# V of a batch loaded once, for its range and for its splits

## The chip, the cores and the metric

The kernel runs on one core of a Trainium2 chip. The metric is device time in microseconds of one execution; the kernel before takes 630.58 us (median of 3 runs, 629.67 to 632.43). The engines have the profile's names: PE (TensorE matmuls; PEld its weight loads), DVE (VectorE), ACT (ScalarE), POOL (GpSimd), SP (the queue that issues nearly all DMAs). Each engine works through its own instructions in the order in which the program lists them, and waits where an operand or a buffer isn't free.

## The reference

Attention with 8 global and 96 local keys and a bias per head (4 batches, 8 heads, 768 positions, 64 per head), then a feed-forward layer on its output. All arrays are float32.

```python
scores = q @ k.transpose(0, 1, 3, 2) / sqrt(D) + bias     # masked to global and local keys
a = softmax(scores);  x = a @ v                           # x -> (3072 tokens, 512)
h = x @ w_in                                              # 512 -> 2048
out = (maximum(h, 0) + alpha * minimum(h, 0)) @ w_out     # 2048 -> 512
```

## The kernel before

**Units.** The 3072 tokens are cut into 12 units u of 256 tokens; units 3b, 3b+1 and 3b+2 make batch b. A unit runs attention for 8 heads (scores `sp`, biased scores `pr` on DVE at L717, exponentials on ACT at L722, products with V `av` at L789), turns its output `xn` into the transposed fp16 pair `xt` (L819), and runs 16 slices f of the feed-forward layer: 12 matmuls `h` (L851), a chain of four operations that makes `g` (ACT L349, DVE L873, ACT L875, DVE L375) and 6 matmuls `o` (L896) that add to the output. Attention of later units is interleaved with the feed-forward of earlier ones. The names carry their numbers: h4_9 is unit 4, slice 9; pt5_1 is unit 5, head 1; xt4 belongs to unit 4.

**Split numbers.** fp32 operands are fed to PE as two fp16 halves (high, and what is left). From unit 2 on V is split too (`load_v`): V of a unit is loaded as `rawv` (two DMAs of 256 KB), multiplied by a scale vs of the batch, and split into `v16` (ACT or DVE at L349/L350 for the high half, DVE at L376 for the low one). Copies of shifted rows, `gp`, are made from `v16` by DMAs (L637).

**The range.** vs is a power of two, found by `v_range` from the largest |V| of the batch: all of V is loaded (six DMAs of 256 KB for batches 1 to 3, into the two `stage` buffers, L456), ACT takes the sums of absolute values (L458, tile `vr`), DVE their maximum (L464, `vmm`), DVE spreads it on a diagonal (L468, `vdg`), PE multiplies that with ones (L470, `vrow`, which gives every partition all 128 maxima), DVE reduces the product (L472), and seven small DVE operations make vs and the output scale osc (L477 to L483). The last four steps have one key. So V of batches 1 to 3 is read from HBM twice.

**What sets the order.** Nothing is written in order by hand: every operation has a key (in slices: 16 per unit) and a modelled cost; `Plan.order` simulates the five engines, and at each moment starts the ready operation with the lowest key on each engine (some operations may go to another engine when the first is behind, `FLEX`). `LAG` is what it adds from the end of one engine's work to the start of what waits for it; for a DMA (SP) 1100 ns. `behind` makes an operation wait in the plan for an earlier one. Each tag in `BUFS` has so many buffers; `rw` (17 of 4 KB a partition) holds raw weights, raw V, `v16`, `gp`, and the `g` of units 3 and later. The program is then emitted in the simulated order, and on the chip each engine keeps it.

Of the kernel before, what the change touches and what calls it, by code (L numbers as in the profile page):

```python
# [20 lines left out]
ALU = mybir.AluOpType  # L21
# [3 lines left out]
P = 128  # L25
# [114 lines left out]
class Plan:  # L140
# [37 lines left out]
    def order(self):  # L178
# [34 lines left out]
        while events:  # L213
# [11 lines left out]
            for e in engines:  # L225
# [35 lines left out]
                heapq.heappush(events, (busy, i, "busy"))  # L261
                heapq.heappush(events, (end + self.LAG[e], i, "free"))
                for j in after[i]:
                    need[j] -= 1
                    for x in engines:
                        own = x == e and e != "SP"
                        at[j][x] = max(at[j][x], end + ((0 if e == "PE" else 60) if own else self.LAG[e]))
# [24 lines left out]
def c_dma(nbytes):  # L292
    return nbytes / 360.0
# [21 lines left out]
WLEAD = 8  # L315
VLEAD = 26.5
VS = 5
# [12 lines left out]
def fast(tc, cn, a):  # L330
    nc = tc.nc
    ctx = ExitStack()
    with ctx:
# [51 lines left out]
        def buf(tag, name, shape, dtype=F32):  # L385
            return Buf(plan, pools[tag], tag, shape, dtype, name)
# [54 lines left out]
        alpha_ = [SimpleNamespace(t=ak.t[:, f : f + 1]) for f in range(NF)]  # L441

        def v_range(b, key):
            m = buf("vm", f"vm{b}", [P, 6])
            for i in range(3):

                t = [buf("w", f"vr{b}_{i}", [P, 2, 512])] * 2 if not b else [
                    buf("stage", f"vr{b}_{i}_{j}", [P, 512]) for j in range(2)]
                if not b:
                    op("SP", key, c_dma(P * 4096), lambda t=t, i=i: nc.sync.dma_start(  # L450
                        out=t[0].t, in_=a["v"][b, 2 * i : 2 * i + 2].rearrange("j p d -> p j d")), w=[t[0]])
                for j in range(2):
                    k = key + 2 * i + j if b else VR
                    x = (lambda t=t, j=j: t[j].t) if b else (lambda t=t, j=j: t[j].t[:, j, :])
                    if b:
                        op("SP", k, c_dma(P * 2048), lambda x=x, i=i, j=j: nc.sync.dma_start(  # L456
                            out=x(), in_=a["v"][b, 2 * i + j]), w=[t[j]])
                    op("ACT", k, c_act(512, ptr=1), lambda x=x, i=i, j=j: nc.scalar.activation(  # L458
                        out=x(), in_=x(), func=AF.Abs, accum_out=m.t[:, 2 * i + j : 2 * i + j + 1]),
                       r=[], w=[(t[j], j), (m, 2 * i + j)])  # L460
            if not b:
                key = VR - 5
            e = buf("vmm", f"vmm{b}", [P, 4])
            op("DVE", key + 6, 80, lambda: v.tensor_reduce(out=e.t[:, 0:1], in_=m.t, axis=AX.X, op=ALU.max), r=[m], w=[e])  # L464

            dg = buf("wf", f"vdg{b}", [P, 3, P])
# [17 lines left out]

            op("DVE", key + 6, 1150, scale, r=[e], w=[vs[b], osc[b]])

# [119 lines left out]
        def load_v(u, key):  # L606
# [5 lines left out]
            def load(name, parts):  # L612
                raw = buf("rw", "raw" + name, [P, 1024])
                for part, rows, j, src in parts:
                    op("SP", key, c_dma(P * 4096 // len(parts)), lambda rows=rows, j=j, src=src: nc.sync.dma_start(
                        out=raw.t.rearrange("p (j k) -> p j k", j=2)[rows, j], in_=src), w=[(raw, part)])
                x = buf("rw", name, [P, 1024])
                for j in range(2):
                    in_ = lambda j=j: raw.t[:, 512 * j : 512 * j + 512]
                    hi, lo = (lambda j=j: view(x)[:, j, 0]), (lambda j=j: view(x)[:, j, 1])  # L620
                    k = key + VS + 0.1 * j
                    mul(k, hi, in_, vs[b], [raw, vs[b]], [(x, (j, 0))], "ACT", 512)
# [505 lines left out]
```

## Time and profile before

| | |
|---|---|
| median of 3 runs | 630.58 us |
| the profiled execution | 631.23 us; its span 629.4 us |
| PE busy | 606.6 us (96%) |
| DVE, ACT, POOL busy | 450.8 (72%), 404.5 (64%), 59.9 us (10%) |
| mean granted clock of PE | 0.994 |
| DMA | 98.78 MB, mean 157 GB/s |

The span runs from the first to the last instruction; 1.8 us of the execution lie around it. A share of busy time is an average over stages: DVE is at 72% over the whole span, and without a gap in one stretch of it. In a timeline row the bracket at the end is the idle time of that engine just before, with what ended it by the profile.

### The profile page before, as it was taken

To read this page: it belongs to the slowest core of one execution; us is meant where nothing else is said; L and a number is where in the kernel's file an instruction comes from. 1 tells how busy PE (TensorE), PEld (TensorE's weight loads), DVE (VectorE), ACT (ScalarE), POOL (GpSimd) and SP (SyncE) were. 2 spreads that over 40 slices of the span, in tenths; PEclk is the share of its full clock that TensorE was granted. 3 is DMA by queue.
4 is the path that set the end of the run, shared out by engine and by line. 5 is a ranking of instruction groups with operands and counts; after the bars stand their busy time and mean duration, and the time that the engine had idled before them with its cause. 6 is when DMAs were issued, how large, how long until landed. Compare 5 with 4: busy or idle time off the path is not lost.

```text
span 629.4 us, 13874 instructions
## 1 busy us (share of the span) xinstructions
PE 606.6 (96%) x5124; PEld 416.7 (66%) x5124; DVE 450.8 (72%) x1318; ACT 404.5 (64%) x1049; POOL 59.9 (10%) x137
## 2 busy tenths in 40 slices
PE   8899999989999999898999999999999999999995
PEld 6787666556667666565666666676666676676663
DVE  5599999995777587585677777787677677656431
ACT  5999999955647466554665775675666665543431
POOL 2001233322111000000000000000000000000000
PEclk9999999999999999998999999999999999999998
DMA  8998664456455655976569558859549647431001
GB/s 310 410 407 270 207 131 107 123 119 156 99 114 130 135 132 153 227 127 153 148 145 216 170 132 179 219 157 194 163 122 195 180 101 139 131 68 34 34 2 39
DMA packets 128844, 98.78 MB, mean 157 GB/s; under 512 B 103168, under 2 KB 103424, under 8 KB 128768
## 3 DMA queue, kind: packets, MB, share of 16 engines
q1 hardware_dynamic: 128624, 97.69, 60.9%
q8 instruction: 42, 0.69, 0.4%
q14 instruction: 34, 0.28, 0.1%
q10 hardware_dynamic: 144, 0.13, 0.1%
HBM read 62.92 MB, written 6.29 MB: 110 GB/s over the span
## 4 chain that ended last, share of the span: by engine, by line
PE 76%; DVE 11%; DMA 7%; issue 2%; ACT 2%; POOL 0%; SPq 0%; ACTq 0%; DVEq 0%; POOLq 0%
PE o L896 32%; PE h L851 32%; PE av L789 5%; PE sp L679 4%; DMA vr<-in_v_dram 2%; DVE wf L533 2%; DVE whl L376 2%; PE sp L711 2%; DMA w<-in_w_dram 1%; DVE whl L538 1%; DVE g L873 1%; DMA rawgp<-in_v_dram 1%; DVE pr L717 1%; DMA pt<-ps 1%; DVE ps L376 1%
## 5 line engine op out<-in xcount | busy, mean ns | idle before, releaser
L851 PE MATMUL h<-xt,whl 128*128 128x256 f16 x2304 | 282.7, 273 | 4.8 <-DVE g L873 4.1
L851 PEld LDWEIGHTS <-whl 128*128 128x128 f16 x2304 | 223.2, 98 | 63.1 <-issue 8.3
L896 PE MATMUL o<-whl,g 128*128 128x512 f16 x864 | 209.0, 380 | 0.0
L349 ACT ACTIVATE g<-h,ak 128x256 f32<-128x256 f32 x170 | 79.7, 469 | 130.6 <-PE h L851 130.3
L873 DVE SCALAR_TENSOR_TENSOR g<-h,g 128x256 f32<-128x256 f32 x192 | 80.4, 420 | 106.5 <-ACT g L349 105.6
L896 PEld LDWEIGHTS <-g 128*128 128x128 f16 x864 | 82.3, 98 | 79.8 <-ACT g L349 5.9
L722 ACT ACTIVATE pr<-pr,sm 128x256 f32<-128x256 f32 (+1 forms) x192 | 92.2, 483 | 4.4 <-DVE sm L717 4.4
L875 ACT CAST g<-g 128x256 f16<-128x256 f32 x144 | 57.6, 400 | 41.7 <-DVE g L873 41.5
L375 DVE TENSOR_TENSOR g<-g 128x256 f16<-128x256 f32 x144 | 60.5, 420 | 30.2 <-ACT g L875 30.1
L717 DVE CUSTOM_DVE_ANT_0 pr<-sp,D 128x256 f32<-128x256 f32 (+1 forms) x192 | 67.4, 394 | 6.2 <-PE sp L711 5.1
L896 PE MATMUL o<-whl,gh 128*128 128x512 f16 x192 | 57.2, 379 | 0.0
L376 DVE SCALAR_TENSOR_TENSOR ps<-pr,ps 128x512 f16<-128x512 f32 (+1 forms) x80 | 52.3, 655 | 5.3 <-ACT ps L349 4.4
L730 POOL TENSOR_TENSOR fin<-fin,sm 128x4 f32<-128x4 f32 x40 | 14.2, 356 | 357.7 <-ACT pr L722 357.4
L375 POOL TENSOR_TENSOR gl<-g,gh 128x256 f16<-128x256 f32 x35 | 30.4, 871 | 91.1 <-ACT gh L875 82.8
L789 PEld LDWEIGHTS <-pt 128*128 128x128 f16 x888 | 31.5, 98 | 8.3 <-DMA pt<-ps 2.0
L722 ACT ACTIVATION_READ_ACCUMULATOR pr<-pr,sm 128x1 f32 x192 | 36.4, 190 | 0.0
L896 PE MATMUL o<-whl,gl 128*128 128x512 f16 x96 | 36.4, 379 | 0.0
L349 ACT ACTIVATE ps<-pr 128x512 f16<-128x512 f32 (+1 forms) x55 | 32.7, 594 | 3.5 <-DMA pt<-ps 2.7
L376 DVE SCALAR_TENSOR_TENSOR x<-raw,x 128x672 f16<-128x672 f32 (+1 forms) x40 | 34.0, 851 | 0.0
L789 PE MATMUL av<-v,pt 128*128 128x64 f16 x480 | 30.2, 193 | 1.9 <-DMA pt<-ps 1.9
L679 PE MATMUL sp<-x 64*128 64x256 f16 (+1 forms) x480 | 31.2, 263 | 0.0
L349 ACT ACTIVATE x<-raw 128x672 f16<-128x672 f32 (+1 forms) x35 | 25.6, 730 | 6.6 <-PE sp L679 6.4
(113 smaller groups left out, 551.8 us busy)
## 6 DMA issues: line engine op xcount, KB each, us to landing
w<-in_w_dram SPq DMA_DIRECT2D x32, 512.0 KB, 8.5
again<-in_w_dram SPq DMA_DIRECT2D x32, 512.0 KB, 4.4
raw<-in_qk_dram SPq DMA_DIRECT2D x28, 336.0 KB, 3.5
out_dram<-os SPq DMA_DIRECT2D x23, 256.0 KB, 2.2
rawv<-in_v_dram SPq DMA_DIRECT2D x20, 256.0 KB, 3.4
vr<-in_v_dram SPq DMA_DIRECT2D x18, 256.0 KB, 3.3
raw<-in_qk_dram SPq DMA_DIRECT2D x12, 272.0 KB, 2.9
gp<-v SPq DMA_DIRECT2D x15, 192.0 KB, 4.0
```

Source lines behind the costliest of these rows:

```text
L349: lambda: nc.scalar.mul(out=out(), in_=src(), mul=by.t if tile_ else by)),
L375: return e.tensor_tensor(out=out(), in0=src(), in1=hi(), op=ALU.subtract)
L376: return e.scalar_tensor_tensor(out=out(), in0=src(), scalar=val(), in1=hi(), op0=ALU.mult, op1=ALU.subtract)
L679: nc.tensor.matmul(sp.t[:, pc : pc + m], lhsT=x.t[rows, qi, 128 * qb : 128 * qb + 128], rhs=x.t[rows, ki, 256 + off : 256 + off + m], star ...
L717: op("DVE", key, c_dve(n) + 10, lambda qb=qb, n=n, dc=dc, pc=pc: v.tensor_tensor_reduce(out=pr.t[:, pc : pc + n], in0=sp.t[:, pc : pc + n] ...
L722: op("ACT", key + 1, c_act(n, ptr=1) + 93, lambda qb=qb, n=n, pc=pc: nc.scalar.activation(out=pr.t[:, pc : pc + n], in_=pr.t[:, pc : pc + ...
L730: op("POOL", key + 3, c_pool(2 * G), lambda: nc.gpsimd.tensor_tensor(out=fin.t[:, : 2 * G], in0=fin.t[:, : 2 * G], in1=sm.t[:, 2 * G : 4 * ...
L789: nc.tensor.matmul(out, lhsT=p_[:, 128 * j : 128 * j + 128], rhs=v_(j), start=m == 0, stop=m == len(ps) - 1)
L851: nc.tensor.matmul(hp.t, lhsT=w.t[:, wi, wc], rhs=x.t[:, NC * xi + c, :], start=n == 0, stop=n == 3 * NC - 1)
L873: op("DVE", key, c_dve(UT), lambda: v.scalar_tensor_tensor(out=g_(), in0=hp.t, scalar=KG, in1=g_(), op0=ALU.mult, op1=ALU.max), r=[hp], w= ...
L875: op("ACT", key, c_act(UT), lambda: nc.scalar.copy(out=gh_(), in_=g_()), r=[rg], w=[rh])
L896: nc.tensor.matmul(o.t, lhsT=g_()[:, tok], rhs=w.t[:, wi, 512:1024], start=f == 0 and n == 0, stop=f == NF - 1 and n == 2)
```

## The change

V of batches 1 to 3 is loaded by three DMAs of 512 KB (`v_load`, key 14 slices before the batch's first unit) into three `rw` buffers, `rawv`, where it stays until each of the batch's units has split its part: `load_v` loads nothing for units 3 to 11. The range has four parts with keys of their own, 9 to 2.5 slices before the unit: `v_sums` (six ACT operations, now into a scratch buffer `vabs`, since V must survive), `v_most` (maximum and diagonal), `v_range` (product, its maximum, the scale). For these batches `behind(plan.mark)` ties each sum, the maximum and the product to the feed-forward slice that was recorded last. For DMAs with a key over 40, `LATE` = 2000 ns stands in place of the lag of 1100 ns in the planner.

```diff
+                lag = LATE if e == "SP" and ops[i][0] > 40 else self.LAG[e]
-VLEAD = 26.5
+LATE = 2000
+        def v_load(b, key):
+            for i in range(3):
+                x = rawv[b, i] = buf("rw", f"rawv{3 * b + i}", [P, 1024]) if b else buf("w", f"vr{b}_{i}", [P, 2, 512])
+                op("SP", key, c_dma(P * 4096), lambda x=x, i=i: nc.sync.dma_start(
+                    out=x.t.rearrange("p (j k) -> p j k", j=2) if b else x.t,
+                    in_=a["v"][b, 2 * i : 2 * i + 2].rearrange("j p k -> p j k")), w=[x])
+        def v_sums(b, i, key):
+            ...
+            y = buf("wf", f"vabs{b}_{i}", [P, 512]) if b else t
+            op("ACT", key, c_act(512, ptr=1), lambda: nc.scalar.activation(
+                out=y.t if b else x(), in_=x(), func=AF.Abs, accum_out=m.t[:, i : i + 1]),
+               r=[t] if b else [], w=[y if b else (t, i % 2), (m, i)])
+            if b:
+                plan.behind(plan.mark)
+        def v_most(b, key):
+            ...
         def v_range(b, key):
-            m = buf("vm", f"vm{b}", [P, 6])
-            for i in range(3):
-            ...
+            e, dg = vmax[b]
             ...
             def load(name, parts):
-                raw = buf("rw", "raw" + name, [P, 1024])
-                for part, rows, j, src in parts:
+                raw = rawv[b, c] if u > 2 else buf("rw", "raw" + name, [P, 1024])
+                for part, rows, j, src in parts if u == 2 else ():
-            jobs.append((min(48 * b - VLEAD - (4 if b > 1 else 0), begin(3 * b) - 0.5) if b else V0, v_range, (b,)))
+            k = begin(3 * b)
+            jobs.append((k - 14 if b else V0, v_load, (b,)))
+            for i in range(6):
+                jobs.append((k - 9 + 0.8 * i if b else VR, v_sums, (b, i)))
+            jobs.append((k - 4 if b else VR + 1, v_most, (b,)))
+            jobs.append((k - 2.5 if b else VR + 2, v_range, (b,)))
```

What the planner makes of it is seen in the order of the built program. First the range of batch 2 in the DVE order of before: maximum, diagonal and the reduction of PE's product stand close together, behind the g chain of slice 7.

```order
L375 TENSOR_TENSOR g4_7_3960<-g4_7_3960 128x256
L376 SCALAR_TENSOR_TENSOR ps5_6_3968<-pr5_6_3919,ps5_6_3968 128x512
L350 TENSOR_SCALAR g4_8_3997<-h4_8_3971,ak_146 128x256
L376 SCALAR_TENSOR_TENSOR ps5_7_3990<-pr5_7_3931,ps5_7_3990 128x512
L464 TENSOR_REDUCE vmm2_4017<-vm2_3125 128x1
L873 SCALAR_TENSOR_TENSOR g4_8_3997<-h4_8_3971,g4_8_3997 128x256
L468 TENSOR_SCALAR vdg2_4020<-ident_58,vmm2_4017 128x128
L738 RECIPROCAL sm5_6_3920<-sm5_6_3920 128x4
L375 TENSOR_TENSOR g4_8_3997<-g4_8_3997 128x256
L472 TENSOR_REDUCE vmm2_4017<-vrow2_4025 128x1
```

In the DVE order of the changed kernel maximum and diagonal follow the g chain of slice 5 (the reduction of the product comes 16 rows further, behind slice 7's g).

```order
L885 SCALAR_TENSOR_TENSOR g4_5_3869<-h4_5_3848,g4_5_3869 128x256
L376 TENSOR_TENSOR g4_5_3869<-g4_5_3869 128x256
L471 TENSOR_REDUCE vmm2_3908<-vm2_3698 128x1
L474 TENSOR_SCALAR vdg2_3912<-ident_58,vmm2_3908 128x128
L885 SCALAR_TENSOR_TENSOR g4_6_3906<-h4_6_3878,g4_6_3906 128x256
```

So the diagonal moves ahead by about two slices on DVE. On PE, before, the product vrow2 stands behind h4_9 and ahead of the values av5_4:

```order
L851 MATMUL h4_9_4004<-xt4_3506,whl9_1268 128x256
L470 MATMUL vrow2_4025<-vdg2_4020,ones_63 128x128
L789 LDWEIGHTS pt5_4_3827
L789 MATMUL av5_4_4029<-gp5_3407,pt5_4_3827 128x64
L789 LDWEIGHTS pt5_4_3827
```

In the changed kernel vrow2 stands on PE behind the second product of o4 with g4_4, which is ahead of h4_8:

```order
L908 LDWEIGHTS g4_4_3826
L908 MATMUL o4_1_3834<-whl4_850,g4_4_3826 128x512
L480 MATMUL vrow2_3966<-vdg2_3912,ones_63 128x128
L801 LDWEIGHTS pt5_4_3828
L801 MATMUL av5_4_3968<-gp5_3394,pt5_4_3828 128x64
```

vrow2 and av5_4 move ahead on PE by h4_8, two o groups and h4_9. The SP queue before, around the transposes xt4 that unit 4's first slice h4_0 reads:

```order
L767 DMA_TRANSPOSE pt5_0_3462<-ps5_0_3400 128x8x128
L662 DMA raw6_4_3474<-in_qk_dram 128x544
L548 DMA again0_0_3485<-in_w_dram 128x512
L767 DMA_TRANSPOSE pt5_1_3488<-ps5_1_3464 128x8x128
L819 DMA_TRANSPOSE xt4_3506<-xs4_0_3478 128x8x128
L819 DMA_TRANSPOSE xt4_3506<-xs4_1_3483 128x8x128
L662 DMA raw6_6_3591<-in_qk_dram 128x544
```

The SP queue of the changed kernel at the same place:

```order
L779 DMA_TRANSPOSE pt5_0_3449<-ps5_0_3387 128x8x128
L674 DMA raw6_4_3461<-in_qk_dram 128x544
L560 DMA again0_0_3472<-in_w_dram 128x512
L450 DMA rawv6_3475<-in_v_dram 128x2x512
L450 DMA rawv7_3492<-in_v_dram 128x2x512
L450 DMA rawv8_3495<-in_v_dram 128x2x512
L831 DMA_TRANSPOSE xt4_3501<-xs4_0_3465 128x8x128
L831 DMA_TRANSPOSE xt4_3501<-xs4_1_3470 128x8x128
L779 DMA_TRANSPOSE pt5_1_3540<-ps5_1_3451 128x8x128
```

Three loads of 512 KB now stand between again0_0 and xt4, and pt5_1 has moved behind xt4. Batch 3's loads stand the same way ahead of xt7. On PE, h4_0 moves behind four o groups (those of g3_13 and g3_14) and ahead of av5_0.

## Rows read from the trace of the kernel before

**Rows 1.** Stretches: us; PE, PEld, DVE, ACT, POOL busy; PEclk; DMA; GB/s.
```profile
20.00:60.00 40.00, 38.47 (x289) 31.25 (x290) 35.27 (x104) 38.41 (x92) 2.75 (x7) 1.00 0.99 371
60.00:140.00 80.00, 74.00 (x607) 49.67 (x606) 79.47 (x186) 67.73 (x159) 24.15 (x31) 1.00 0.55 136
260.00:300.00 40.00, 35.32 (x307) 23.34 (x305) 28.19 (x92) 22.62 (x64) 1.52 (x6) 0.96 0.71 157
300.00:620.00 320.00, 320.00 (x2742) 216.89 (x2741) 216.11 (x650) 189.21 (x495) 13.01 (x44) 1.00 0.57 134
```
**Rows 2.** Waits of PE: line, releaser, us in total, times, longest.
```profile
PE h L851 <- DVE g L873: 4.1, 7, 1.5
PE vrow L470 <- DVE vdg L468: 3.3, 2, 1.8
```
**Rows 3.** Timeline around the product of batch 2: start, us, engine, line.
```profile
257.68 0.42 DVE L375 TENSOR_TENSOR g<-g 128x256 f16<-128x256 f32 x1 [2.54 <-ACT g L875]
...
261.37 1.47 PE L851 MATMUL h<-xt,whl 128*128 128x256 f16 x12
...
266.62 0.63 ACT L458 ACTIVATE vr<-vr 128x512 f32<-128x512 f32 x1 [1.33 <-DMA vr<-in_v_dram]
...
267.78 0.28 DVE L468 TENSOR_SCALAR vdg<-ident,vmm 128x128 f32<-128x128 f32 x1
...
268.20 0.46 PE L470 MATMUL vrow<-vdg,ones 128*128 128x128 f32 x2 [2.76 <-DVE sm L738]
```
**Rows 4.** Timeline around the product of batch 1.
```profile
127.71 0.46 PE L470 MATMUL vrow<-vdg,ones 128*128 128x128 f32 x2 [1.84 <-DVE vdg L468]
```
**Rows 5.** DVE groups, by form.
```profile
L376 DVE SCALAR_TENSOR_TENSOR v<-rawv,vs,v 128x512 f16<-128x512 f32 x20 | 15.9, 809 | 0.0
L350 DVE TENSOR_SCALAR g<-h,ak 128x256 f32<-128x256 f32 x22 | 10.6, 481 | 3.1 <-PE h L851 2.8
```
**Rows 6.** Timeline from unit 5's transposes to unit 6's first values.
```profile
280.11 5.08 SPq L819 DMA_TRANSPOSE xt<-xs  x2
...
286.00 1.23 SPq L767 DMA_TRANSPOSE pt<-ps  x1
...
290.59 0.26 PE L789 MATMUL av<-v,pt 128*128 128x64 f16 x3 [1.92 <-DMA pt<-ps]
...
290.86 2.47 PE L851 MATMUL h<-xt,whl 128*128 128x256 f16 x12
293.12 2.19 PE L896 MATMUL o<-whl,g 128*128 128x512 f16 x6
295.14 1.04 PE L851 MATMUL h<-xt,whl 128*128 128x256 f16 x8
```
**Rows 7.** The stretch behind that wait; columns as in rows 1.
```profile
292.00:294.00 2.00, 2.00 (x10) 1.09 (x8) 0.60 (x3) 0.47 (x1) 0.00 (x0) 0.50 0.51 98
```
**Rows 8.** Timeline from unit 4's transposes (xt4) to h4_0 and h4_1.
```profile
229.76 3.76 SPq L819 DMA_TRANSPOSE xt<-xs  x2
...
237.39 0.25 PE L789 MATMUL av<-gp,pt 128*128 128x64 f16 x3
...
238.09 1.48 PE L851 MATMUL h<-xt,whl 128*128 128x256 f16 x12
239.40 1.46 PE L896 MATMUL o<-whl,g 128*128 128x512 f16 x6
240.69 1.47 PE L851 MATMUL h<-xt,whl 128*128 128x256 f16 x12
```
**Rows 9.** Stretches of the DMAs there; columns as in rows 1.
```profile
228.00:235.00 7.00, 7.00 (x55) 4.43 (x53) 5.11 (x17) 3.23 (x10) 0.00 (x0) 1.00 1.06 241
235.00:236.00 1.00, 1.00 (x12) 0.89 (x10) 1.00 (x4) 1.00 (x6) 0.00 (x0) 1.00 0.01 1
```
**Rows 10.** Timeline of xt7 and h7_0.
```profile
377.98 2.61 SPq L819 DMA_TRANSPOSE xt<-xs  x2
...
387.59 0.60 PE L851 MATMUL h<-xt,whl 128*128 128x256 f16 x4
```

More of the change, by code (lines that the diff above doesn't have):

```diff
@@ L261, in order @@
                 heapq.heappush(events, (busy, i, "busy"))
-                heapq.heappush(events, (end + self.LAG[e], i, "free"))
+                lag = LATE if e == "SP" and ops[i][0] > 40 else self.LAG[e]
+                heapq.heappush(events, (end + lag, i, "free"))
                 for j in after[i]:
@@ L266, in order @@
                         own = x == e and e != "SP"
-                        at[j][x] = max(at[j][x], end + ((0 if e == "PE" else 60) if own else self.LAG[e]))
+                        at[j][x] = max(at[j][x], end + ((0 if e == "PE" else 60) if own else lag))
                     if not need[j]:
@@ L441, in fast @@
         alpha_ = [SimpleNamespace(t=ak.t[:, f : f + 1]) for f in range(NF)]
-        def v_range(b, key):
-            m = buf("vm", f"vm{b}", [P, 6])
-            for i in range(3):
[L447 to L466, printed above, removed]
@@ new lines, in fast @@
+        vmax, rawv = {}, {}
+        def v_load(b, key):
[5 more added lines that the diff above has]
+        def v_sums(b, i, key):
+            if i == 0:
+                vmax[b] = buf("vm", f"vm{b}", [P, 6])
+            m, t = vmax[b], rawv[b, i // 2]
+            y = buf("wf", f"vabs{b}_{i}", [P, 512]) if b else t
+            x = (lambda: t.t[:, 512 * (i % 2) : 512 * (i % 2) + 512]) if b else (lambda: t.t[:, i % 2])
+            op("ACT", key, c_act(512, ptr=1), lambda: nc.scalar.activation(
[3 more added lines that the diff above has]
+                plan.behind(plan.mark)
@@ new lines, in v_most @@
+        def v_most(b, key):
+            m, e = vmax[b], buf("vmm", f"vmm{b}", [P, 4])
+            dg = buf("wf", f"vdg{b}", [P, 3, P])
+            vmax[b] = e, dg
+            op("DVE", key, 80, lambda: v.tensor_reduce(out=e.t[:, 0:1], in_=m.t, axis=AX.X, op=ALU.max), r=[m], w=[e])
+            if b:
+                plan.behind(plan.mark)
+            op("DVE", key, c_dve(P, True, True), lambda: v.tensor_scalar(
+                out=dg.t[:, 0, :], in0=ident, scalar1=e.t[:, 0:1], scalar2=None, op0=ALU.mult), r=[e], w=[dg])
@@ L467, in v_range @@
+        def v_range(b, key):
+            e, dg = vmax[b]
             row = buf("sp" if b == 1 else "av", f"vrow{b}", [P, 512])
-            op("DVE", key + 6, c_dve(P, True, True), lambda: v.tensor_scalar(
-                out=dg.t[:, 0, :], in0=ident, scalar1=e.t[:, 0:1], scalar2=None, op0=ALU.mult), r=[e], w=[dg])
-            op("PE", key + 6, 230, lambda: nc.tensor.matmul(
+            op("PE", key, 230, lambda: nc.tensor.matmul(
                 row.t[:, :P], lhsT=cn["ones"], rhs=dg.t[:, 0, :], start=True, stop=True), r=[dg], w=[row])
-            op("DVE", key + 6, c_dve(P), lambda: v.tensor_reduce(
+            if b:
+                plan.behind(plan.mark)
+            op("DVE", key, c_dve(P), lambda: v.tensor_reduce(
@@ L483, in scale @@
                 v.tensor_scalar(out=osc[b].t, in0=osc[b].t, scalar1=1.0 / (WI * WO * KG), scalar2=None, op0=ALU.mult)
-            op("DVE", key + 6, 1150, scale, r=[e], w=[vs[b], osc[b]])
+            op("DVE", key, 1150, scale, r=[e], w=[vs[b], osc[b]])
         raww, whl = {}, {}
@@ L620, in load @@
                     hi, lo = (lambda j=j: view(x)[:, j, 0]), (lambda j=j: view(x)[:, j, 1])
-                    k = key + VS + 0.1 * j
+                    k = key + (VS if u == 2 else 1) + 0.1 * j
                     mul(k, hi, in_, vs[b], [raw, vs[b]], [(x, (j, 0))], "ACT", 512)
@@ L632, in load_v @@
             g = gp[u] = buf("rw", f"gp{u}", [P, 1024])
-            key += VS + 1
+            key += 2
             def move(i, part, to, first, last, src, j, parts):
@@ L951, in fast @@
             if u > 1:
-                jobs.append((begin(u) - VL, load_v, (u,)))
+                jobs.append((begin(u) - (VL if u == 2 else 0.1), load_v, (u,)))
             for qb in range(2):
```

## The prediction

> **What bounds the kernel now.** I read the stretches first [rows 1]. The reader is to see three stages. Between 60 and 140 us DVE is busy for 79.5 of 80 us and PE for 74.0: there VectorE sets the pace, and PE loses 6.0 us. Between 260 and 300 us PE is busy 35.3 of 40, although every other engine has room: it loses 4.7 us. Between 300 and 620 us PE has no gap at all, so nothing done there can gain anything; it can only add a gap. Between 20 and 60 us PE loses 1.5 us while ACT is busy 38.4 of 40 and DMA share is 0.99, so that stage has several limits at once.
>
> Then the waits of PE [rows 2]: 4.1 us in seven waits for g (the DVE-bound stage), and 3.3 us in two waits of the product vrow for its diagonal (1.8 of it in batch 1, the rest in batch 0, at the start). The timeline shows what PE lost between 260 and 300 us. The product of batch 2 waited 2.76 us [rows 3]: the profile names an sm, but the diagonal vdg ends only at 268.06, just before the product starts, and the diagonal was late because ACT's last sum had waited for the last load of V until 266.62. The values of unit 6 waited another 1.92 us for a transposed pt [rows 6]. 2.76 and 1.92 are the 4.68 us that this stretch loses. After the second wait PE ran slowly: the granted clock is 0.50 [rows 7], the lower of its two levels, 1.2 instead of 2.4 GHz. One h group took 2.26 us (290.86 to 293.12) and one o group 2.02 (to 295.14) [rows 6], where 1.31 and 1.29 are usual [rows 8]: 0.95 + 0.73 = 1.7 us.
>
> So all that a change of V's handling could give back after the start is 1.5 + 6.0 + 4.7 + 1.7 = 13.9 us, and it touches only part of that.
>
> **The change part by part.** The sum is made against the profiled execution's own 631.2 us.
>
> *The product of batch 2.* V lies in SBUF long before its sums, and the sums no longer wait for two buffers to come free and be loaded again. In the new DVE order the diagonal stands right behind g4_5. In the old trace g4_5's last operation starts at 257.68, after a wait of 2.54 for an ACT that was itself held by the sums' loads [rows 3]. In the new PE order the product stands just ahead of h4_8, which PE reached at 261.37 [rows 3]. The operation takes 0.42, the diagonal 0.28 [rows 3], the maximum no more than that, so the diagonal is there at about 258.6, some 2.8 us ahead of PE even if nothing on ACT gets quicker. The wait of 2.76 goes. What could be late next on PE is av5_4, which moved ahead with the product by h4_8, two o groups and h4_9, some 3.9 us; the SP order doesn't put its transposes later, and the row of before gives PE no wait there beyond the product's. Bounds: 0 to -2.8; I take -2.8, since the row shows the margin.
>
> *The product of batch 1.* It waited 1.84 us [rows 4], in the stage where DVE has no gap. PE's next groups there wait for g in any case, so what the product gives back is largely waited for elsewhere. By the order up to unit 1's last g, eight operations come to DVE (five scalings by alpha, a low half of V, two others) and eight go (scalings of V, probabilities and others). At 0.48 us each [rows 5] that is nothing; if all that come were of the 0.81 us form and all that go of the 0.48 us form it were 8 x 0.33 = +2.6, the other way round -2.6. The sums on ACT stay six, with the same shape. Bounds -1.8 (the whole wait; DVE can't give more to a PE that is 92% busy) to +2.6; I take -0.5.
>
> *The stall of unit 6.* Its pt was issued at 286.00, because SP had spent 5.08 us on the two transposes of xt5 [rows 6], where xt7 took 2.61 [rows 10]. In the new order two copies of gp6 go out ahead of pt6_0 and a raw load, not behind them, and no loads of V stand before. That thins the queue ahead of xt5, but the same transposes follow each other. Bounds: 0 to -3.6 (wait 1.92 and clock 1.7); I take a third, -1.2, nearer to nothing because the order of PE around this place is unchanged.
>
> *The loads in one block.* Three loads of 512 KB, 1.57 MB, now stand on SP ahead of xt4. Before, xt4 was issued from 229.76 on [rows 8] and the DMAs were done by 235.0 [rows 9]. The block takes 4.2 us at the 371 GB/s of a stretch of loads [rows 1] and 6.5 us at the 241 GB/s of the very stretch [rows 9], so xt4 is there at 239.2 to 241.5. PE reached h4_0 at 238.09; four o groups are now ahead of it (two pairs of 1.29) and the values av5_0 (0.70) behind it [rows 8], so it comes at 238.1 + 2.6 - 0.7 = 240.0. PE waits 0 to 1.5 us. At xt7 the old slack is larger: issue ends at 380.6 [rows 10], data 1.5 us later if as at xt4, 382.1. Block and one load of 0.52 MB (1.4 to 2.2) behind its first half make 387.7 to 390.8, less some 1.3 us because the block is issued earlier than xt7 was. h7_0 comes at 387.59 [rows 10] + three o groups 1.9 - 0.7 = 388.8: 0 to 0.7 us. Behind the block on SP wait pt5_1 and pt8_1, whose values stand behind h4_0 and h7_0 too. Together 0 to +2.2; I take +0.4, since the loads' own rate is the nearer row for a block that is loads alone. The Trainium skill, in "DMA: Bandwidth & Descriptors" (section "Queues, rings and completion order"), says that each DMA engine takes descriptors from a ring in ring order; by that xt4 pays for the block in full, as reckoned here, and no row of before shows a transpose behind so much data. Were the rings not in order, this term would be 0.
>
> *The start.* Two loads of 256 KB leave the stream of weights: 0.52 MB at 371 GB/s [rows 1], -1.4 us at most. On the other side the keys of batch 0's range differ, and ACT, DVE and PE take unit 1's attention ahead of the first weights; the first h comes later, the tail of attention earlier. PE's loss is only 1.5 us between 20 and 60 [rows 1], so it can hardly gain more; a loss of the same size bounds the other side. I take -0.3.
>
> *LATE.* The planner now assumes that units 4 and later get their DMA results 0.9 us later. This costs no instruction; it puts consumers further behind. PE had no gap from 300 on [rows 1], so it gains nothing there, and what it moves on PE is seen in the order at h4_0 and h7_0 only. 0.
>
> *Traffic.* 4.7 MB less is read (nine units, two loads of 0.26 MB). At a DMA share of 0.55 to 0.71 after 60 us [rows 1] this is off the path.
>
> Sum: -2.8 - 0.5 - 1.2 + 0.4 - 0.3 = -4.4, that is 631.2 - 4.4 = 626.8 in the profiled execution. That execution lay 0.65 us above the median of the runs shown, so the runs should give 626.2. All bounds together make -9.6 to +6.3.
>
> **The rivals.**
>
> *Only the product's wait goes* (628.2). The stall of unit 6 comes back in full, the DVE-bound stage takes back what batch 1 gives: 631.2 - 2.8 + 0.4 - 0.65. For it: order of PE behind h4_10 is unchanged, and DVE has 0.5 us of room in 80 [rows 1]. Against it: less is queued ahead of xt5.
>
> *The block holds up the transposes: slower* (636). The place is SP ahead of xt4 and xt7, the price a wait of PE at h4_0 and h7_0 and a fall of the clock behind each. xt5 shows that SP can be held for 2.5 us by a full queue (5.08 against 2.61) [rows 6, 10]. With 2.5 on top of the 6.5 us, xt4 comes at 244.0 and PE waits 4.0; xt7 comes at 382.1 + 9.0 + 2.2 - 1.3 = 392.0 and PE waits 3.2. Each with 1.7 us of the lower clock: 10.6 - 4.8 = +5.8 on 630.6. It decides from about 2.4 us of lateness at both places, which with the clock eats the 4.8 us gained. Against it: a block of loads alone should run nearer to 371 than to 241 GB/s.
>
> *The change doesn't do what it says* (630.6). The sums now write to the scratch tag wf, shared with the sizes of the weights, and each is tied behind a slice; if they are late, PE waits for the diagonal as before, and the rest of the sum is noise around nothing. Against it: the margin of 2.8 us.
>
> **How the numbers follow.** Forecast 0.63, only the product 0.22, not what it says 0.07, slower 0.08. The forecast's own range is 623.0 to 628.0 (the stall of unit 6 gone wholly, or the start costing 1.5). For 8 in 10 I leave out the slower case and the outermost of the others: 622.8 to 630.2. 0.5% is 3.15 us, about what a measurement of this kernel can tell from no change. Faster by more, under 627.4: nine tenths of the forecast and a quarter of the first rival, 0.62. Slower by more: 0.08. Between: 0.30.
>
> **What would show it.** Right: no idle PE ahead of the three products; PE busy in 260 to 300 us up from 35.3 towards 39; granted clock 1.0 through 300 us; h4_0 and h7_0 with waits under 1.5 us; PE without a gap from 300 on. Wrong: PE waiting at an h for xt, at the product for vdg, at an av for pt, each with a clock under 1 behind it; or more than 7.5 us lost by PE between 20 and 140 us.

## The result, and the profile after

The changed kernel takes 624.44 us (median of 4 runs, 622.68 to 624.69), the kernel before 630.34 (4 runs, 629.67 to 632.43): a ratio of 0.9895, 95% interval 0.9865 to 0.9924. The forecast was 626.2, range 622.8 to 630.2. The profiled execution takes 624.44 us, its span 622.7: 6.8 us less than the one of before, where I had worked out 4.4. Medians and ratios, here and below, leave out three executions that took more than twice as long as the rest (two of e9, one of the kernel before).

The same stretches as in [rows 1], with two more; the columns are us, then PE, PEld, DVE, ACT and POOL busy, PEclk, DMA share, GB/s.

```profile
0.00:20.00 20.00, 17.11 (x105) 14.18 (x105) 9.96 (x53) 13.21 (x45) 3.56 (x17) 1.00 0.91 327
20.00:60.00 40.00, 39.92 (x296) 32.08 (x297) 36.05 (x107) 38.66 (x91) 4.01 (x7) 1.00 0.96 361
60.00:140.00 80.00, 73.98 (x607) 49.63 (x606) 79.66 (x185) 68.16 (x157) 25.18 (x32) 1.00 0.51 134
140.00:260.00 120.00, 119.30 (x1068) 80.74 (x1066) 83.95 (x250) 73.60 (x208) 13.14 (x31) 1.00 0.62 139
260.00:300.00 40.00, 39.72 (x362) 26.97 (x360) 30.87 (x98) 24.91 (x68) 2.37 (x8) 1.00 0.68 145
300.00:620.00 320.00, 315.89 (x2694) 213.50 (x2692) 211.76 (x632) 184.28 (x480) 12.47 (x42) 1.00 0.53 125
```

PE lost 1.53 us between 20 and 60 us and loses 0.08 now; 4.68 between 260 and 300 us, now 0.28; in the stage where DVE has no gap it lost 6.00 and loses 6.02. (Behind 300 us PE has no gap; the 4 us missing in that row lie behind its end.) The waits of PE, beside [rows 2]; us in total, times, longest:

```profile
PE h L863 <- DVE g L885: 4.4, 7, 1.8
PE sp L691 <- DVE xn L810: 0.8, 1, 0.8
PE h L863 <- DMA xt<-xs: 0.7, 1, 0.7
PE vrow L480 <- DVE vdg L474: 0.5, 1, 0.5
```

Of the three waits for a diagonal, 6.1 us together, 0.5 is left (batch 1), but new waits for xn and more for g stand beside it. The timeline at batch 2's product, as in [rows 3], and at unit 6, as in [rows 6]; start, us, engine, line:

```profile
255.72 0.15 DVE L471 TENSOR_REDUCE vmm<-vm 128x1 f32<-128x6 f32 x1
255.91 0.29 DVE L474 TENSOR_SCALAR vdg<-ident,vmm 128x128 f32<-128x128 f32 x1
261.14 0.38 PE L480 MATMUL vrow<-vdg,ones 128*128 128x128 f32 x2
...
271.97 1.18 SPq L649 DMA_DIRECT2D gp<-v  x2
273.74 1.24 SPq L779 DMA_TRANSPOSE pt<-ps  x1
...
276.77 2.77 SPq L831 DMA_TRANSPOSE xt<-xs  x2
281.22 1.21 SPq L779 DMA_TRANSPOSE pt<-ps  x1
285.73 0.26 PE L801 MATMUL av<-v,pt 128*128 128x64 f16 x3 [0.28 <-DMA pt<-ps]
...
286.00 1.47 PE L863 MATMUL h<-xt,whl 128*128 128x256 f16 x12
287.31 1.46 PE L908 MATMUL o<-whl,g 128*128 128x512 f16 x6
288.60 1.47 PE L863 MATMUL h<-xt,whl 128*128 128x256 f16 x12
```

The diagonal is there 5 us ahead of PE; before, it ended just as the product began. Unit 6's values wait 0.28 us and not 1.92, and xt5's transposes are issued in 2.77 us and not 5.08. The clock does not fall: one h and one o group take 2.60 us (286.00 to 288.60), before 4.28 (290.86 to 295.14 in [rows 6]). The row that answers [rows 7], shortly behind the wait:

```profile
288.00:290.00 2.00, 2.00 (x17) 1.51 (x16) 0.85 (x2) 0.41 (x1) 0.00 (x0) 1.00 0.75 154
```

The timeline at the block of loads ahead of xt4, as in [rows 8]:

```profile
228.13 1.46 SPq L450 DMA_DIRECT2D rawv<-in_v_dram  x3
229.69 7.13 SPq L831 DMA_TRANSPOSE xt<-xs  x2
239.76 1.47 PE L863 MATMUL h<-xt,whl 128*128 128x256 f16 x12
```

SP is held at xt4 for 7.13 us (before 3.76), yet h4_0 has no bracket: PE did not wait. The times of xt4's two transposes from issue to landing (shortest, median, longest), before and then in the changed kernel:

```profile
DMA to landing us min/median/max: 3.6/4.1/4.5
DMA to landing us min/median/max: 5.7/7.3/8.9
```

The shortest is that of the second transpose, issued at 232.3 before and at 233.8 now; so xt4 is there at 235.9 before and at 239.4 now, 0.3 us ahead of h4_0.

What each part gave is read from the time at which PE starts the same piece of work, not from PE's idle time: a stretch can lose idle time and get no further for it, when PE is counted as busy for longer. The rows of before, then of the changed kernel: the first values of unit 0 (`av`), the transposes of unit 1's output (`xp`), and an h behind the stage in which DVE has no gap.

```profile
13.37 1.55 PE L789 MATMUL av<-first,pt 128*128 128x64 f32 x12
52.42 1.04 PE L827 MATMUL xp<-ident,xn 128*128 128x128 f32 x8
152.27 1.47 PE L851 MATMUL h<-xt,whl 128*128 128x256 f16 x12
...
13.61 1.55 PE L801 MATMUL av<-first,pt 128*128 128x64 f32 x12
51.92 1.04 PE L839 MATMUL xp<-ident,xn 128*128 128x128 f32 x8
152.05 1.47 PE L863 MATMUL h<-xt,whl 128*128 128x256 f16 x12
```

| part | before | changed | difference, us |
|---|---|---|---|
| up to `av`, where PE's order is the same | 13.37 | 13.61 | +0.24 |
| `av` to `xp` | 39.05 | 38.31 | -0.74 |
| `xp` to that h | 99.85 | 100.13 | +0.28 |
| that h to unit 6's wait | 136.40 | 133.40 | -3.00 |
| unit 6's wait | 1.92 | 0.28 | -1.64 |
| one h and one o group behind it (the clock) | 4.28 | 2.60 | -1.68 |

The sum is -6.54; the rest, up to the 6.8, lies behind the last row and around the span. Of the 3.00 us the product's wait is 2.76. PE's idle time up to 60 us fell by 1.7 us (3.16 + 1.53 before, 2.89 + 0.08 now), but PE was only 0.5 us further on at `xp`: the rest of the 1.7 was counted as busy.

### The profile page after: what moved, and what is told of

Read it like the earlier page. It is cut to its first block, busy times and chain, and to the rows that moved or that the text cites. A ratio compares the mean times of both kernels' runs of the same rounds, so it can differ in the third digit from the quotient of the medians.

```text
span 622.7 us, 13832 instructions
## 1 busy us (share of the span) xinstructions
PE 605.9 (97%) x5124; PEld 417.1 (67%) x5124; DVE 452.3 (73%) x1322; ACT 402.8 (65%) x1045; POOL 60.7 (10%) x137
## 4 chain that ended last, share of the span: by engine, by line
PE 80%; DVE 12%; DMA 3%; ACT 2%; issue 1%; POOL 0%; ACTq 0%; SPq 0%; POOLq 0%; DVEq 0%
PE o L908 34%; PE h L863 34%; PE av L801 4%; PE sp L691 4%; DVE wf L545 2%; DVE whl L377 2%; PE sp L723 2%; DVE whl L550 1%; DVE g L885 1%; ACT pr L734 1%; DVE x L377 1%; DMA rawgp<-in_v_dram 1%; DVE pr L729 1%; DVE ps L377 1%; DMA pt<-ps 1%
## 5 line engine op out<-in xcount | busy, mean ns | idle before, releaser
L350 ACT ACTIVATE g<-h,ak 128x256 f32<-128x256 f32 x164 | 77.3, 471 | 133.3 <-PE h L863 132.1
L742 POOL TENSOR_TENSOR fin<-fin,sm 128x4 f32<-128x4 f32 x40 | 13.6, 341 | 351.2 <-ACT pr L734 346.9
```

The costliest lines, as they stand in the source:

```text
L350: lambda: nc.scalar.mul(out=out(), in_=src(), mul=by.t if tile_ else by)),
L742: op("POOL", key + 3, c_pool(2 * G), lambda: nc.gpsimd.tensor_tensor(out=fin.t[:, : 2 * G], in0=fin.t[:, : 2 * G], in1=sm.t[:, 2 * G : 4 * ...
```

## The experiments

Twelve kernels, each against runs of the kernel before on the same chip. The column av–xp is the time from unit 0's first values to the transposes of unit 1's output, as above. PE's losses in the columns behind it are stretch minus busy time in the profiled execution. In some executions PE reaches unit 0's first scores up to a microsecond sooner and then waits there 0.5 to 1.0 us for operands; these waits are taken off the column 0–60.

| kernel | median us | ratio to before, 95% | av–xp | 0–60 | 60–140 | 140–260 | 260–300 |
|---|---|---|---|---|---|---|---|
| before | 630.3 | 1 | 39.05 | 4.7 | 6.0 | 0.5 | 4.7 |
| changed | 624.44 | 0.9895 (0.9865–0.9924) | 38.31 | 3.0 | 6.0 | 0.7 | 0.3 |
| e1 old start order | 625.64 | 0.9937 (0.991–0.9963) | 39.05 | 4.8 | 5.8 | 1.6 | 0.0 |
| e2 two loads back | 623.85 | 0.989 (0.987–0.9911) | 38.31 | 3.2 | 5.4 | 0.2 | 0.3 |
| e3 copies late | 623.2 | 0.988 (0.9855–0.9905) | 38.31 | 3.2 | 5.9 | 0.4 | 0.3 |
| e4 one key | 625.89 | 0.992 (0.9898–0.9941) | 38.30 | 3.0 | 7.0 | 0.0 | 0.4 |
| e5 copies swapped | 624.62 | 0.989 (0.986–0.992) | 38.31 | 3.2 | 5.9 | 0.4 | 1.3 |
| e6 staged sums | 623.67 | 0.9878 (0.9849–0.9908) | 38.31 | 3.2 | 5.9 | 0.3 | 0.3 |
| e7 before, range early | 625.52 | 0.9908 (0.9879–0.9937) | 39.05 | 4.7 | 6.0 | 0.1 | 1.6 |
| e8 V loaded twice | 625.63 | 0.9911 (0.9881–0.9941) | 38.30 | 3.0 | 5.5 | 1.8 | 0.2 |
| e9 before, start order | 628.56 | 0.9972 (0.9938–1.0005) | 38.30 | 3.2 | 5.1 | 0.3 | 2.6 |
| e10 before, both keys | 624.63 | 0.9904 (0.9872–0.9935) | 38.31 | 3.2 | 5.1 | 0.6 | 2.4 |
| e11 LATE 1100 | 625.06 | 0.992 (0.9893–0.9946) | 38.31 | 3.1 | 5.8 | 1.2 | 0.0 |
| e12 less on DVE | 623.75 | 0.9901 (0.987–0.9932) | 38.30 | 3.0 | 5.8 | 0.4 | 0.5 |

Many intervals overlap, so what tells the theories apart is the trace of each, more than a median.

**The start: e1, e2, e9.** The sums of batch 0 have key -23, and so have the exponentials of unit 0's seventh head. Ties go by the place on the planner's list; the rewritten code lists batch 0's sums later, so the exponentials now come first, and PE's order differs up to some 93 us, with those of DVE and ACT. e1 puts the tie back, e2 the two loads:

```diff
 e1
-                jobs.append((k - 9 + 0.8 * i if b else VR, v_sums, (b, i)))
+                jobs.append((k - 9 + 0.8 * i, v_sums, (b, i)) if b else (V0, lambda i, _: v_sums(0, i, VR), (i,)))
 ...
 e2
+        def v_extra(b, key):
+            for j in range(2):
+                x = buf("stage", f"vx{b}_{j}", [P, 512])
+                op("SP", key, c_dma(P * 2048), lambda x=x, j=j: nc.sync.dma_start(
+                    out=x.t[:, :512], in_=a["v"][b, j, :, :512]), w=[x])
 ...
+        jobs.append((21.5, v_extra, (1,)))
```

> The changed kernel, with one difference: the four parts of batch 0's range are put on the planner's list at the place where they stood before, ahead of unit 0's attention, and with the old keys. Its sums then come ahead of the exponentials of unit 0's seventh head, which have the same key (-23), and PE, DVE and ACT follow the order of before through the start; the loads stay those of the changed kernel. Theory O (the order of the start is what gave back 1.7 us between 0 and 60 us): PE loses 4.7 us there as before (3.2 and 1.5) and not 3.0, the product of batch 0 waits about 1.5 us again, time 624.4 + 1.7 = 626.1, 625.3 to 627. Rival L (two loads of 256 KB fewer ahead of the weights gave it back): PE loses 3.0 us, 624.4, 623.8 to 625. The later stages are planned anew behind the other start; what they lose is read apart.

> The changed kernel, with two loads of 256 KB of V put back on SP at the two places of the start where the kernel before had them, into buffers that nobody reads. The orders of PE, DVE and ACT are those of the changed kernel. Rival L (the loads were what gave back 1.7 us): PE loses 4.4 to 4.7 us between 0 and 60 us, since 0.52 MB at the 361 GB/s of that stretch is 1.45 us, and the time is 625.8 to 626.1. Theory O (the order of the start gave it back): PE loses 3.0 to 3.3 us, 624.4 to 624.8.

From e1's waits of PE up to 60 us, that of batch 0's product for its diagonal, which the changed kernel has not, and from its timeline its h4_0:

```profile
PE vrow L480 <- DVE vdg L474: 1.5, 1, 1.5
241.27 1.48 PE L863 MATMUL h<-xt,whl 128*128 128x256 f16 x12 [1.25 <-DMA xt<-xs]
```

The stretch of e2, with 375 GB/s between 20 and 60 us, where the changed kernel has 361:

```profile
20.00:60.00 40.00, 39.74 (x293) 31.55 (x293) 36.20 (x107) 38.67 (x91) 4.02 (x7) 1.00 1.00 375
```

With the old tie the loss is that of before, 4.8 us, and av to xp takes 39.05 us again; with the old loads they stay at 3.2 and 38.31, and the time does not rise. So rival L is out and the order of the start is the cause, by a tie that nobody had set. But theory O has its size wrong: the order is worth 0.74 us of PE's progress and not 1.7. By the h behind the stage of DVE even this is hardly left: e1 starts it at 152.15, the changed kernel at 152.05, both with first values at 13.6; and xp to that h takes from 99.16 (e2) to 100.13 us (changed kernel) in executions with one and the same order, so what remains of the 0.74 there is not resolved. e1's median is 1.8 to 2.4 above e2 and e3 on the same chip, about as expected, but not for the reason expected: in its trace h4_0 waits 1.25 us for xt4, where the changed kernel does not, though PE's order is the same from 93 us on. Why xt4 comes later there stays open.

e9 is the other direction, on the kernel before:

```diff
-VR = -23
+VR = -22.99
```

> The kernel before, with one number changed: the key of batch 0's range is -22.99 and not -23, so that the exponentials of unit 0's seventh head come ahead of its sums. PE, DVE and ACT then take the changed kernel's order through the start. Theory O (that order alone gave back 1.8 us in the start): PE loses 2.9 to 3.3 us between 0 and 60 us and not 4.7, no wait of batch 0's product, both stalls of batch 2 as before, 630.7 - 1.8 = 628.9, 628.2 to 629.8. Rival: without the rest of the change the time is given back before 140 us, where DVE has no gap: 630.3 to 631.2.

PE's loss up to 60 us is 3.2, as theory O says, and av to xp takes 38.30 us: the tie alone does it. The time is inconclusive: single runs lay from 625.25 to 631.93 (at mean granted clocks of 0.997 and 0.991), and the interval holds both 1 and the expected 0.997.

**The product of batch 2: e4, e6, e7.** What took its wait away: the separate points, V lying in SBUF, or only the time in hand? e4 gives back one key for the last steps, e6 feeds the sums of batches 2 and 3 through the two stage buffers again, e7 is the kernel before with the range earlier:

```diff
 e4
-            jobs.append((k - 4 if b else VR + 1, v_most, (b,)))
+            jobs.append((k - 2.5 if b else VR + 1, v_most, (b,)))
 e6
+            if b > 1:
+                t = buf("stage", f"vr{b}_{i}", [P, 512])
+                op("SP", key, c_dma(P * 2048), lambda t=t: nc.sync.dma_start(out=t.t, in_=a["v"][b, i]), w=[t])
 ...
 e7
-            jobs.append((min(48 * b - VLEAD - (4 if b > 1 else 0), begin(3 * b) - 0.5) if b else V0, v_range, (b,)))
+            jobs.append((min(48 * b - VLEAD - (10 if b > 1 else 0), begin(3 * b) - 0.5) if b else V0, v_range, (b,)))
```

> The changed kernel, with the maximum and the diagonal of batches 1 to 3 at the key of the product and the scale (2.5 slices ahead of the unit, not 4), so that the last steps have one key as before; loads and sums are those of the changed kernel. In the order maximum and diagonal of batch 2 come about 13 DVE instructions later, and h4_8 stands ahead of the product and not behind. Theory A (what took the wait of the product away is that V lies in SBUF in time): no idle time over 0.3 us ahead of the product of batches 2 and 3, PE loses under 1 us between 260 and 300 us, 624.0 to 625.2. Rival B (the separate points took it away): the product of batch 2 waits 1 to 2.8 us again, with one more for batch 3, 626 to 628. For batch 1 both say that PE loses 5.5 to 6.5 us between 60 and 140 us, since DVE has no gap there wherever the product stands.

> The changed kernel, with the sums of batches 2 and 3 fed as before: six loads of 256 KB of their own through the two stage buffers, each buffer loaded again when its sum is done. V for the splits is still loaded once and ahead, and the four parts keep their separate keys. Rival R (late loads hold ACT at the sums, and that alone brought both stalls of batch 2): the product waits 1.5 to 2.8 us, the values of unit 6 wait 1 to 2 us more with a fall of the granted clock, PE loses 3 to 5 us between 260 and 300 us, 627 to 630. Theory S (the separate points are what counts): PE loses under 1 us there, 623.5 to 625.

> The kernel before, with one number changed: the range of batches 2 and 3 is 6 slices earlier, with its loads through the two stage buffers, one key for its last steps, and V loaded again for the splits. Theory M (the gain in batch 2 is a matter of time in hand alone): no wait of the product of batch 2, unit 6's values wait under 0.6 us, PE loses under 1.2 us between 260 and 300 us, while the start loses 4.7 us up to 60 us as before: 630.6 - 4.4 - 0.7 = 625.5, 624.8 to 626.5. Rival N (loads through two buffers hold ACT wherever the sums stand, so V has to lie in SBUF): ACT waits over 3 us for loads of V, PE loses 2 us or more at another place, 628 to 631.

In e4 batch 2's product doesn't wait, and PE loses 0.4 us between 260 and 300 us. In e6's timeline ACT's one wait for a load of V and the product's wait are small:

```profile
255.11 0.63 ACT L464 ACTIVATE vr<-vr 128x512 f32<-128x512 f32 x1 [0.99 <-DMA vr<-in_v_dram]
262.90 0.46 PE L483 MATMUL vrow<-vdg,ones 128*128 128x128 f32 x2 [0.21 <-DVE vdg L477]
```

With the new keys, loads through two buffers are in time, so the premise of rival R (ACT held by late loads) did not come about. In e7 no product of batch 2 or 3 waits, and 625.5 is what theory M gave. The changed kernel, e6 and e7 have only an earlier range in common; loading once (not in e7) and the separate points (not in e4, e7) are not needed to remove the 2.76 us. What failed of M is unit 6, below.

e4 shows where a separate point does count, in batch 1. Its diagonal comes later on a DVE that has no gap; the timeline:

```profile
127.47 0.77 PE L480 MATMUL vrow<-vdg,ones 128*128 128x128 f32 x2 [2.36 <-DVE vdg L474]
```

PE had been busy for 4.92 of 5 us at the full clock; behind the wait it runs near the lower level (0.5 is 1.2 of 2.4 GHz) for some 4 us, as e4's stretches show:

```profile
120.00:125.00 5.00, 4.92 (x33) 2.96 (x31) 5.00 (x13) 4.09 (x10) 1.23 (x3) 1.00 0.28 52
...
127.00:129.00 2.00, 1.53 (x7) 1.25 (x8) 1.97 (x8) 0.00 (x0) 0.00 (x0) 0.56 0.00 0
129.00:131.00 2.00, 2.00 (x11) 1.33 (x10) 1.21 (x7) 0.10 (x1) 0.00 (x0) 0.58 0.67 125
```

Both theories had said 5.5 to 6.5 us of loss there; it was 7.0, with the clock on top, and e4's median is 2.0 to 2.7 above e2 and e3.

**The stall of unit 6: e3, e5, e7.** e3 moves the two copies of gp6 back to right ahead of xt5 by their key; e5 does it behind the planner's back, so that only SP's order changes.

```diff
 e3
-            key += 2
+            key += 2.5 if u == 6 else 2
 e5
-        for i in self.order():
 ...
+        order = [i for i in order if i not in self.late]     # late: the two copies of gp6
+        at = order.index(self.to)                            # to: the first transpose of xt5
+        for i in order[:at] + late + order[at:]:
             self.way[i]()
```

> The changed kernel, with the two copies of gp6 put on SP where they stood before: behind the transposes pt6_0 and the load raw7_4, right ahead of the two transposes of xt5. On PE only h5_0 changes places with the next operation. Theory Q (the stall of unit 6 went because the queue ahead of xt5 was thinned by the copies): the issue of xt5 takes 4.5 to 5.1 us and not 2.8, pt6_1 is issued about 2.3 us later, the values of unit 6 wait 1.5 to 2.5 us, the granted clock falls behind that wait, and the time is 626.5 to 628. Rival E (everything there is simply earlier, by the 2.8 us of the product's wait or by other orders, and the place of the copies doesn't matter): the issue of xt5 stays under 3.2 us, the wait under 0.8 us, 624.2 to 625.

> The changed kernel, with nothing but two DMAs moved on SP behind the planner's back: the two copies of gp6 go out behind pt6_0 and raw7_4, right ahead of the two transposes of xt5, as before the change; PE, DVE and ACT keep the changed kernel's order to the last instruction. (In the run with the copies late, the planner also put h5_0 ahead of unit 6's values, which covers 1.3 us.) Theory Q (the place of the copies sets how long SP is held at xt5): the issue of xt5 takes 4.1 to 5.1 us and not 2.8, pt6_1 goes out 1.4 to 2.3 us later against PE's work, the values of unit 6 wait 1.6 to 2.6 us and not 0.3, and the time is 1.3 to 4 us above that of the runs with PE's changed order (623.2 to 624.4): 625 to 628. Rival R (unit 6 stalled because the sums had held ACT for loads of V, and with them the operations behind; the copies don't matter): wait under 0.8 us, 623 to 624.8.

e3 told little: xt5's issue took 4.15 us, but the planner had put h5_0 ahead of unit 6's values, whose 1.3 us covered it. The timeline of e5:

```profile
274.61 1.18 SPq L654 DMA_DIRECT2D gp<-v  x2
275.90 3.53 SPq L838 DMA_TRANSPOSE xt<-xs  x2
281.15 1.21 SPq L786 DMA_TRANSPOSE pt<-ps  x1
285.72 0.26 PE L808 MATMUL av<-v,pt 128*128 128x64 f16 x3 [1.28 <-DMA pt<-ps]
```

and of e7, where the product doesn't wait and the copies stand as before:

```profile
275.99 4.81 SPq L819 DMA_TRANSPOSE xt<-xs  x2
286.16 0.26 PE L789 MATMUL av<-v,pt 128*128 128x64 f16 x3 [1.61 <-DMA pt<-ps]
```

with e7's stretch, at the full clock:

```profile
260.00:300.00 40.00, 38.39 (x354) 26.19 (x353) 29.04 (x88) 24.00 (x67) 2.37 (x8) 1.00 0.69 143
```

Moving two copies costs 1.0 of the 1.64 us (wait 1.28 and not 0.28; the median, 624.62, lies under the 625 to 628 expected), and without the product's wait the stall is still there in e7. So theory Q holds for most of the wait, below the size that I had expected (1.6 to 2.6), and rival R is out. The other 0.6 us was not separated. Nor do the copies account for the clock's 1.68 us: with them back in place the clock stayed up in e5, and in e7 too.

**Both keys on the kernel before: e10**, which is the kernel before with e7's and e9's numbers.

> The kernel before, with two numbers changed: the key of batch 0's range (-22.99), and the range of batches 2 and 3 6 slices earlier. V is still loaded twice, the last steps have one key, the sums go through the two stage buffers. Theory M (time in hand for the range and the order of the start are all of the gain but the place of gp6's copies): 625.5 of the run with the earlier range - 1.8 = 623.7, 623.0 to 624.6; PE loses 3.0 us up to 60 us, the product of batch 2 does not wait, unit 6's values still wait 1.3 to 1.9 us. Rival (loading once is worth 1.5 us or more by itself): 625 to 626.

Of its waits of PE, and of its stretches, that of unit 6's values and the one behind it:

```profile
PE av L789 <- DMA pt<-ps: 2.4, 1, 2.4
```

```profile
286.00:288.00 2.00, 1.86 (x16) 1.49 (x17) 1.27 (x4) 0.82 (x2) 0.00 (x0) 0.50 0.59 154
```

Two numbers in the kernel before give 0.9904, the whole change 0.9895: no difference that these intervals show. The profiled execution was the longest of the nine (626.59; median 624.63), with unit 6's wait at 2.4 and the clock at its lower level behind it. The median is at the upper edge of theory M's 623.0 to 624.6, and the rival's 625 to 626 is not excluded by the interval of the ratio.

**Loading once: e8.** V of units 3 to 11 is loaded a second time for the splits. Its timeline, behind the expectation, shows the second load of unit 4's V ahead of xt2.

```diff
-                raw = rawv[b, c] if u > 2 else buf("rw", "raw" + name, [P, 1024])
-                for part, rows, j, src in parts if u == 2 else ():
-                    op("SP", key, ...
+                raw = buf("rw", "raw" + name, [P, 1024])
+                for part, rows, j, src in parts:
+                    op("SP", key - (3.9 if u > 2 else 0), ...
```

> The changed kernel, with V of units 3 to 11 loaded a second time for the splits (nine loads of 512 KB as two of 256 KB each, 3.9 slices ahead of the split), as before; V for the range is still loaded ahead in one block, and the order of PE is the changed kernel's. Theory: traffic counts for nothing at a DMA share of 0.5 to 0.7, 623.2 to 624.8, and PE loses what it does in the changed kernel, within 0.7 us in each stage. Rival: the loads delay transposes that PE or DVE wait for; 4.7 MB at 361 GB/s are 13 us of DMA time, and if a tenth of it falls on waits of PE for xt or pt, 625 to 626.

```profile
132.01 1.07 SPq L627 DMA_DIRECT2D rawv<-in_v_dram  x2
138.44 2.65 SPq L831 DMA_TRANSPOSE xt<-xs  x2
142.97 2.79 PE L863 MATMUL h<-xt,whl 128*128 128x256 f16 x24 [1.44 <-DMA xt<-xs]
```

and the last of these rows in the changed kernel:

```profile
142.93 2.79 PE L863 MATMUL h<-xt,whl 128*128 128x256 f16 x24 [0.70 <-DMA xt<-xs]
```

By the time the rival is nearer: the median is 1.0 to 2.0 above e5 and e6 on the same chip. Its mechanism is not shown. PE waits 1.44 us for xt2 (0.70 in the changed kernel) and loses 1.8 between 140 and 260 us (0.7), but the h behind the wait starts at the same time in both, 142.97 and 142.93: PE had only got there sooner. The order of DVE and ACT changed between 131 and 148 us too, so the loads alone are not proved to be the cause.

**LATE: e11.**

```diff
-LATE = 2000
+LATE = 1100
```

> The changed kernel with the planner's lag for DMAs of units 4 and later put back from 2000 to 1100 ns. Some six PE groups (o groups of units 3 and 6) and a dozen DVE instructions change places. Theory: the number costs and gives nothing, 623.2 to 624.6, no new wait of PE over 0.5 us behind 140 us. Rival: it put consumers of transposes far enough behind to cover them; without it PE waits 1 us or more for xt or pt, and the time is 625 to 626.5.

```profile
238.53 1.47 PE L863 MATMUL h<-xt,whl 128*128 128x256 f16 x12 [0.89 <-DMA xt<-xs]
```

The rival, nearly at its size (the line is of e11's timeline): h4_0 waits 0.89 us for the xt4 behind the block of loads. In the changed kernel the two o groups of g3_14 stand ahead of h4_0, 1.3 us of work, and the wait is gone. Not all of the 0.89 us stays: between 260 and 300 us e11 loses nothing, the changed kernel 0.3.

**Less work for DVE: e12**, the attempt at a faster kernel.

```diff
-            return ... + first[1] > FLEX[e] * own[1]
+            return ... + first[1] > (dict(ACT=1.0, DVE=2.5).get(e, 1) if 5 < ops[i][0] < 34 else FLEX[e]) * own[1]
```

> The changed kernel, and for operations with keys from 5 to 34 the planner gives ACT the scaling of the weights' high half as soon as DVE is behind by its cost, and DVE takes work from ACT only when ACT is behind by 2.5 times the cost: five scalings of 0.52 us and two of 0.475 us leave DVE and one of 0.43 us comes, 3.1 us less in the stage in which DVE has no gap. Theory D (DVE sets the pace between 60 and 140 us, so PE's loss of 6 us follows DVE's work): PE loses 3 to 4.5 us there, 621.0 to 623.0, faster than both kernels. Rival (ACT, busy for 68 of 80 us, is as late as DVE then, and the chain of four operations behind each h waits for it): 623.5 to 625.5.

Two stretches of e12:

```profile
60.00:140.00 80.00, 74.17 (x606) 49.54 (x605) 79.45 (x182) 70.30 (x163) 24.19 (x32) 1.00 0.53 137
140.00:260.00 120.00, 119.62 (x1070) 80.81 (x1068) 81.24 (x243) 74.60 (x210) 14.81 (x34) 1.00 0.60 137
```

DVE is as full as before up to 140 us; the work that left it shows only behind (81.24 and not 83.95 us busy). Theory D fell: less work in that stage let later work move in, and PE's loss stayed at 5.8. The time, 623.75, is in the rival's range; that ACT takes DVE's place as the limit is not shown, since DVE still has no gap there and ACT has 10 us. No kernel here is faster than the changed one by more than the intervals allow.

## Why the prediction was right, and where not

- *The product of batch 2*, -2.8: it gave 2.76, with 5 us of margin. But "V lies in SBUF long before its sums" was not what it took: e6 and e7 remove the wait without that.
- *The stall of unit 6*, -1.2: the term most mis-sized. The wait gave 1.64 and the clock 1.68, together 3.3, near the bound of 3.6. I had named what thins the queue (two copies of gp6 out of the way of xt5) and then taken a third, "since the order of PE around this place is unchanged". PE's order had no part in it; the copies' place on SP makes 1.0 us (e5). With the product's wait gone and the copies left, the clock stayed up in e7 and fell in e10, so what brought back the clock's part is open.
- *The start*, -0.3: the order gave 0.74 by xp, and the loads that I had put first nothing (e2). The row was there: [rows 2] put 3.3 us on two waits for a diagonal, 1.8 of them in batch 1, so 1.5 on batch 0's product, and the order showed that other work now stands ahead of it. That wait went, and about half of it was lost again to longer busy time.
- *The product of batch 1*, -0.5: not seen. The wait fell from 1.84 to 0.55, yet PE's loss stayed at 6.0, as argued for most of it, and xp to the h behind the stage took 0.28 us more, within what executions of one order differ by. Against the changed kernel's own order the separate point is worth some 2 us (e4), a cost that kept off rather than a gain.
- *The block of loads*, +0.4, and *LATE*, 0: together 0, by two errors. Without LATE h4_0 waits 0.9 us for it (e11). xt4 is there at 239.4, the early end of the forecast's 239.2 to 241.5, but again by two errors: it had landed at 235.9 before and not at 235.0, where the DMAs' share falls, and the block cost it 3.5 us and not 4.2 to 6.5. By the Trainium skill's ring order ("DMA: Bandwidth & Descriptors", "Queues, rings and completion order") xt4 pays for the block in full, and this trace agrees in the main: 239.4 against the 235.9 of before.
- *Traffic*, 0: against the kernel before nothing shows; within the changed order loading twice costs 1 to 2 us (e8), its cause not separated.

Two sums of the prediction do not come out. The forecast's own range was to start with unit 6's stall gone wholly; that is 2.4 us below 626.2, so 623.8 and not 623.0. And the slower rival was to need 2.4 us of lateness at two places; with 1.7 us of clock behind each, as it reckons, 0.7 would have eaten the 4.8. At h4_0 there was none.

The profiled execution came out 2.4 us below its forecast: unit 6's stall gave 2.1 us more than its term and the block cost 0.4 less, while batch 1 and the start together gave 0.6 less (0.24 of it lost by chance ahead of the first values). That the errors cancelled in part, and that the median came nearer to its forecast (1.8 us), is luck. The largest term of the forecast, the product, was right in its size, and in that the diagonal would be there in time.

## What to carry to other kernels

Where a planner sets the order, look first at what the change moves elsewhere: a tie of two keys moved PE's first 52 us by 0.7 us. Read what a change gives from the time at which the engine starts the same piece of work, not from its idle time: up to 60 us PE's idle time fell by 1.7 us and its work came 0.5 sooner. Ask of a wait that goes whether it needs the change or only more time in hand, and try the one number on the old kernel (e7, e10). Taking work from a full engine does not shorten its stage when work that was planned for later moves in (e12).

## What the runs showed that was not expected

Not every wait of PE is followed by a lower clock, and not by its length alone. Behind 2.76 us at batch 2's product of before the granted clock stayed at 1.00, as the stretch below shows; behind 1.92 us at unit 6, 22 us later, it was 0.50 [rows 7]. Behind 2.36 us (e4) and 2.4 us (e10) it fell, behind 1.61 us (e7) and 1.28 us (e5) it did not. What decides it stays open. The stretch of the kernel before, behind its product of batch 2, columns as above:

```profile
270.00:272.00 2.00, 2.00 (x20) 1.38 (x19) 1.50 (x6) 0.41 (x1) 0.00 (x0) 1.00 0.89 131
```

The first values of unit 0 start between 12.45 us (e2) and 13.62 us (e1) though PE's order up to there is the same: differences of a microsecond between single profiled executions say nothing of a change. From there to xp the same order takes the same time to 0.01 us, in three traces with the old order (39.05) and eleven with the new one (38.30 to 38.31).
